# Two attention blocks on one core: division halves, phi(q) chains and other dense chains laid among one another by a new rule, and block A's last q and k ahead of its values

## The chip, the cores and the metric

The kernel runs on one core of a Trainium2 chip. The metric is the device time of one execution in microseconds; the median of three runs of the kernel before is 288.62 us (287.77, 288.62 and 296.04). Profiles are of one profiled execution, and all places in time below count from the first instruction of that execution.

## The reference

Two blocks with inputs of their own, each with x of 2048 tokens by 640, wqkv of 640 by 1920 and wo of 640 by 640, all bf16. Both have 32 heads of 20. Block A is causal attention in a sliding window of 256 keys; block B is linear attention.

```python
# A: q, k, v = split(x @ wqkv)
scores = einsum("bhqd,bhkd->bhqk", q, k) * 20 ** -0.5
scores = where((0 <= i - j) & (i - j < 256), scores, -1e9)
a = (softmax(scores) @ v) @ wo
# B: q, k, v = split(x @ wqkv)
phi = lambda t: where(t > 0, t + 1, exp(t)) + 1e-6
kv = einsum("bhsd,bhse->bhde", phi(k), v);  z = sum_s phi(k)
num = phi(q) @ kv;  den = phi(q) . z + 1e-6
b = (num / den) @ wo
out = concatenate([a, b], axis=-1)
```

## The kernel before

The tokens are cut into four superblocks of 512. The order of the instructions on every engine is the order in which the program writes them; no scheduler moves them.

**The main loop** walks over 90 units, numbered 0 to 89: units 0 to 17 belong to superblock 0 of block A, 18 to 41 to superblock 1, 42 to 65 to 2, 66 to 89 to 3. A unit writes the scores of one tile on TensorE (`scores`, line 485: keys by queries for four heads, into the one S_ps buffer of four banks), their Exp on ScalarE (line 493, one instruction of 128x2048), and the masks on GpSimd (line 507). The values of a tile (`values`, line 529, 16 short matmuls) are written two units after its scores. In every third unit VectorE normalizes the result of a group of four heads (lines 551 and 552). After that, each unit takes dense matmuls from a generator called `fill` for as many columns as a constant rate gives it (334,400 columns over 90 units, so 3,716 a unit), so dense matmuls stand between the values of one unit and the scores of the next. What the rate leaves over is written behind unit 89, and then the last output projection of block A (`a_out_last`).

**The dense work** comes in chains. A chain is a row of accumulating matmuls into one PSUM bank; a pool `dps` gives three banks to all of them, and when a chain is written it takes a bank that is free at that place of the program. One engine's step or more then reads the bank, and only after the last of them can another chain use it. The kinds, with the letters used below:

- E: a q or k chain of block A (`a_qk`, five matmuls of 512 columns, line 194), evicted by one copy on VectorE (`evac`, line 185). Two of these groups, of five chains each, make q and k of a superblock. They go to DRAM and come back in a padded layout (`bounce`: a write, and four reads for each of q and k, on SP's queue).
- V: a value chain (`v_proj`, five matmuls of 320 columns), evicted in the same way.
- Q: a phi(q) chain of block B (`b_q`, five of 512 columns). `phi` reads the bank twice: an Exp on ScalarE (line 203), and, after a step on the Exp's result (line 207), a VectorE step that takes the larger of the input and 0 and adds the Exp (line 210). These two VectorE steps are not written at once: they wait in a list `later`, and `flush` writes them behind the next eviction, phi or division.
- N: a division half (`b_num`, half of the heads for 128 tokens, three short matmuls against kv_bd, line 436). VectorE adds 1e-6 to the denominators, takes reciprocals and multiplies (lines 445, 448, 449), and the bank is free after the multiplication. After both halves of 128 tokens a DMA transposes the result (otokB) into oT_B, on SP's queue. A superblock has eight halves. oT_B takes the buffers of block A's xA, of which there are two.
- O: an output chain (`wo_proj`, four of 512 columns by five, then one bank with the 128 columns left of all four token blocks, 20 short matmuls), evicted by one copy on VectorE; the finished superblock goes out by a DMA on GpSimd's queue.

Each generator ends a chain by yielding an `End`, and gives a count of columns before it for each matmul. `even(a, na, b, nb, lead)` alternates the chains of two generators: `nb` chains of `b` evenly among `na` chains of `a`, `b` first where `lead` is set. In `fill`, `early` stands for block A's last values and then its last q and k (superblock 3); `outs` for the output projections of superblocks 0 to 2, A and B by turns. The part of `fill` that the change touches begins behind `b_kv(3)`, the last sum of phi(k) and values, in unit 43.

Of the kernel before, what the change touches and what calls it, by code (L numbers as in the profile page):

```python
# [9 lines left out]
P = 128  # L10
# [11 lines left out]
TPS = SB // P  # L22
# [30 lines left out]
def kernel(  # L53
# [10 lines left out]
    nc = tc.nc  # L64
    _, S, D = A_x.shape
    KT = D // P
# [109 lines left out]
    def flush():  # L176

        while later:
            later.pop(0)()

    def evac(dst, src, to=None):
        if to == "A":
            nc.scalar.activation(out=dst, in_=src, func=ACT.Copy)
        else:
            nc.vector.tensor_copy(out=dst, in_=src)  # L185
        flush()

    def bank():
        return dps.tile([P, SB], F32, name="dense")

    def chain(dst, lhs, rhs, n):

        for kt in range(KT):
            nc.tensor.matmul(  # L194
                dst, lhsT=lhs(kt), rhs=rhs(kt), start=(kt == 0), stop=(kt == KT - 1)
            )
            if kt < KT - 1:
                yield n

    def phi(dst, src, view=lambda t: t[:]):  # L200

        e = sp.tile([P, SB], BF16, name="e")
        nc.scalar.activation(out=view(e), in_=src, func=ACT.Exp)  # L203
        flush()

        def rest():
            nc.vector.tensor_scalar(  # L207
                out=e[:], in0=e[:], scalar1=1e-6, scalar2=1.0 + 1e-6, op0=ALU.add, op1=ALU.min
            )
            nc.vector.scalar_tensor_tensor(  # L210
                out=dst, in0=src, scalar=0.0, in1=view(e), op0=ALU.max, op1=ALU.add
            )

        later.append(rest)
# [4 lines left out]
    def even(a, na, b, nb, lead=False):  # L219


        def one(g):
            for c in g:
                yield c
                if isinstance(c, End):
                    break

        done = 0
        for i in range(na):
            while lead and done < nb and done * na <= i * nb:  # L230
                done += 1
                yield from one(b)
            yield from one(a)
            while not lead and done * na < (i + 1) * nb:
                done += 1
                yield from one(b)
        yield from a


    xA, xB = {}, {}  # L240
    q_pad, k_pad, v_tok = {}, {}, {}
# [3 lines left out]
    def bounce(n, s, st, dst):  # L245


        scratch = tc.dram_tile([D, SB], BF16, name=f"{n}_scr{s}")
        eng = nc.scalar if s == 0 else nc.sync
        eng.dma_start(out=scratch.rearrange("(c p) n -> p c n", p=P), in_=st[:])  # L250
        sv = scratch.rearrange("(g j d) n -> j d g n", j=4, d=DH)

        def reads():
            for j in range(4):
                nc.sync.dma_start(out=dst[32 * j : 32 * j + DH, :, :], in_=sv[j])

        return reads

    def a_qk(s, between=()):
        for n, base in (("q", 0), ("k", D)):  # L260
            st = stp.tile([P, KT, SB], BF16, name="st")
            for c in range(KT):
                ps = bank()
                yield from chain(
                    ps[:],
                    lambda kt: w_sb["A"][:, kt, base + c * P : base + (c + 1) * P],
                    lambda kt: xA[s][:, kt, :],
                    SB,
                )
                evac(st[:, c, :], ps[:])  # L270
                if c == KT - 1:
                    pad, pl, name = (q_pad, qp, "qpad") if n == "q" else (k_pad, kp, "kpad")
                    pad[s] = pl.tile([P, NG, SB], BF16, name=name)
                    if n == "q":
                        q_reads = bounce(n, s, st, pad[s])
                        for g in between:
                            yield from g
                    else:
                        late_reads[s] = bounce(n, s, st, pad[s])
                        q_reads()  # L280
                yield End(SB)

    def hook(gen, n, fn):

        for i, c in enumerate(gen):
            if i == n:
                fn()
            yield c

    def v_proj(n, xt, dst):  # L290
        hh = H // 2
        for tb in range(TPS):
            for i in range(2):
                ps = bank()
                yield from chain(
                    ps[:, 0 : hh * DH],
                    lambda kt: xt[:, kt, tb * P : (tb + 1) * P],
                    lambda kt: w_sb[n][:, kt, 2 * D + i * hh * DH : 2 * D + (i + 1) * hh * DH],
                    hh * DH,
                )  # L300
                evac(
                    dst[:, tb, i * hh : (i + 1) * hh, 0:DH],
                    ps[:, 0 : hh * DH].rearrange("p (h d) -> p h d", d=DH),
                )
                yield End(hh * DH)

    def a_v(s):
        v_tok[s] = vp.tile([P, TPS, H, HV], BF16, name="vA")
        nc.gpsimd.memset(v_tok[s][:, :, :, DH:HV], 1.0)
        yield from v_proj("A", xA[s], v_tok[s])  # L310
# [86 lines left out]
    for i in range(2):  # L397
        parts = []
# [7 lines left out]
    oT_B = {}  # L406
# [3 lines left out]
    def b_q(s):  # L410
        xt = xB[NS + s]
        pq = pqp.tile([P, KT, SB], BF16, name="phi")
        pq_of[s] = pq
        for c in range(KT):
            ps = bank()
            yield from chain(
                ps[:],
                lambda kt: w_sb["B"][:, kt, c * P : (c + 1) * P],
                lambda kt: xt[:, kt, :],
                SB,  # L420
            )
            phi(pq[:, c, :], ps[:])
            yield End(SB)

    def b_num(s):
        flush()
        pq = pq_of[s]
        oT_B[s] = xp.tile([P, KT, SB], BF16, name="xA")
        for tb in range(TPS):
            ot = rp.tile([P, D], BF16, name="otokB")  # L430
            for i in range(2):
                ps = bank()
                ov = ps[:, 0 : hh * HV].rearrange("p (h e) -> p h e", e=HV)
                parts = half_parts[i]
                for n, (c, ho, nh, col) in enumerate(parts):
                    nc.tensor.matmul(  # L436
                        ov[:, col : col + nh, :],
                        lhsT=pq[:, c, tb * P : (tb + 1) * P],
                        rhs=kv_bd[:, c, ho : ho + nh, :],
                        start=(n == 0),  # L440
                        stop=(n == len(parts) - 1),
                        skip_group_check=True,
                    )
                den = sp.tile([P, hh, 1], F32, name="denB")
                nc.vector.tensor_scalar_add(
                    out=den[:], in0=ov[:, :, DH:HV], scalar1=1e-6
                )
                nc.vector.reciprocal(out=den[:], in_=den[:])
                nc.vector.tensor_tensor(  # L449
                    out=ot[:, i * hh * DH : (i + 1) * hh * DH].rearrange(  # L450
                        "p (h e) -> p h e", e=DH
                    ),
                    in0=ov[:, :, 0:DH],
                    in1=den[:].to_broadcast([P, hh, DH]),
                    op=ALU.mult,
                )
                flush()
                yield End(3 * 150)
            nc.sync.dma_start_transpose(
                out=oT_B[s][:, :, tb * P : (tb + 1) * P], in_=ot[:]  # L460
            )

    def b_out(s):
        yield from wo_proj("B", oT_B[s], s, D)
# [102 lines left out]
    def a_out(s):  # L567
        yield from wo_proj("A", oT_A[s], s, 0)
# [29 lines left out]
    def seq(*gens):  # L598
        for g in gens:
            yield from g  # L600
# [23 lines left out]
    def k_reads(s, gen):  # L624
        return hook(gen, 8, lambda: late_reads[s]())

    early = seq(a_v(3), a_qk(3))
    outs = seq(a_out(0), b_out(0), a_out(1), b_out(1), a_out(2), b_out(2))
    fill = seq(
        a_qk(1, between=(load("B", 1),)),  # L630
# [10 lines left out]
        k_reads(2, a_v(2)),  # L641
        b_kv(3),
        load("B", NS + 1),
        even(b_q(0), KT, early, 2),
        load("B", NS + 2),
        even(b_num(0), 2 * TPS, early, 2 * TPS, lead=True),
        early,
        k_reads(3, b_q(1)),
        load("B", NS + 3),
        even(b_num(1), 2 * TPS, outs, 2 * TPS, lead=True),  # L650
        even(b_q(2), KT, outs, 2),
        even(b_num(2), 2 * TPS, outs, 2 * TPS, lead=True),
        even(b_q(3), KT, outs, 2),
        even(b_num(3), 2 * TPS, outs, 2 * TPS, lead=True),
        outs,
        b_out(3),
    )
# [60 lines left out]
```

## Time and profile before

| | |
|---|---|
| median of the runs | 288.62 us |
| the profiled execution | 289.15 us |
| its span, first to last instruction | 287.3 us |
| TensorE busy | 272.2 us (95%) |
| ScalarE busy | 199.9 us (70%) |
| VectorE busy | 181.4 us (63%) |
| GpSimd busy | 163.9 us (57%) |
| granted TensorE clock | 1.000 |
| start of units 43, 47, 60, 70, 89 | 146.94, 157.71, 191.69, 217.65, 267.28 |

A unit's start is the start of its first scores matmul in the order of time. Busy times of TensorE count a matmul from its start to a modelled end; matmuls overlap, so a row of five with 512 columns starts one every 0.216 us though each is listed with 0.38.

### The profile page before, as it was taken

To read this page: it belongs to the slowest core of one execution; us is meant where nothing else is said; L and a number is where in the kernel's file an instruction comes from. 1 tells how busy PE (TensorE), PEld (TensorE's weight loads), DVE (VectorE), ACT (ScalarE), POOL (GpSimd) and SP (SyncE) were. 2 spreads that over 40 slices of the span, in tenths; PEclk is the share of its full clock that TensorE was granted. 3 is DMA by queue.
4 is the path that set the end of the run, shared out by engine and by line. 5 is a ranking of instruction groups with operands and counts; after the bars stand their busy time and mean duration, and the time that the engine had idled before them with its cause. 6 is when DMAs were issued, how large, how long until landed. Compare 5 with 4: busy or idle time off the path is not lost.

```text
span 287.3 us, 8258 instructions
## 1 busy us (share of the span) xinstructions
PE 272.2 (95%) x3512; PEld 157.1 (55%) x3512; DVE 181.4 (63%) x409; ACT 199.9 (70%) x227; POOL 163.9 (57%) x212
## 2 busy tenths in 40 slices
PE   7999988998999999999998989998999999999995
PEld 7644554664665654565664644444555464545653
DVE  0666645756765754546664885457867787677861
ACT  2000058987989888879988768897788878986402
POOL 2000039666666666776689646665766767665620
PEclk9999999999999999999999999999999999999999
DMA  7997699999272062273053542179954155022576
GB/s 247 292 321 202 163 248 176 281 144 159 63 112 59 17 94 94 62 149 67 3 116 72 114 48 72 45 171 134 145 127 72 56 86 138 3 94 48 133 167 204
DMA packets 66676, 35.91 MB, mean 125 GB/s; under 512 B 50800, under 2 KB 65264, under 8 KB 66640
## 3 DMA queue, kind: packets, MB, share of 16 engines
q1 hardware_dynamic: 63792, 27.04, 46.7%
q0 software_dynamic: 1536, 7.05, 9.0%
q10 hardware_dynamic: 1312, 1.31, 1.4%
q8 instruction: 27, 0.44, 0.7%
q14 instruction: 9, 0.07, 0.1%
HBM read 12.45 MB, written 10.49 MB: 80 GB/s over the span
## 4 chain that ended last, share of the span: by engine, by line
PE 71%; DVE 8%; DMA 6%; ACT 6%; POOL 5%; issue 2%; SPq 0%; POOLq 0%
PE dense L194 45%; PE O_ps L529 13%; PE S_ps L485 9%; ACT p L493 4%; POOL p L507 3%; DMA k_scr<-st 2%; DMA kpad<-k_scr 2%; DMA oT<-otokA 2%; PE dense L146 1%; DVE phi L210 1%; DVE otokA L552 1%; DVE osb L185 1%; PE dense L377 1%; POOL kv_bd L163 1%; PE dense L436 1%
## 5 line engine op out<-in xcount | busy, mean ns | idle before, releaser
L507 POOL TENSOR_SCALAR_AFFINE_SELECT p<-p 128x512 bf16<-128x512 bf16 (+2 forms) x178 | 148.1, 833 | 108.1 <-ACT p L493 100.6
L493 ACT ACTIVATE p<-S_ps 128x2048 bf16<-128x2048 f32 x90 | 168.8, 1875 | 49.4 <-PE S_ps L485 49.1
L529 PEld LDWEIGHTS <-p 128*128 128x128 bf16 x1440 | 42.4, 96 | 20.8 <-issue 15.8
L529 PE MATMUL O_ps<-vA,p 128*128 128x21 bf16 x1440 | 51.1, 173 | 1.9 <-POOL p L507 1.9
L194 PE MATMUL dense<-wB,xB 128*128 128x320 bf16 (+2 forms) x320 | 49.2, 298 | 0.1
L194 PE MATMUL dense<-xA,wA 128*128 128x512 bf16 x200 | 46.1, 379 | 0.0
L185 DVE CAST st<-dense 128x512 bf16<-128x512 f32 x40 | 27.4, 690 | 19.9 <-PE dense L194 19.5
L485 PE MATMUL S_ps<-qpad,kpad 20*128 20x256 bf16 (+2 forms) x736 | 36.3, 269 | 2.6 <-issue 1.3
L185 DVE CAST osb<-dense 128x512 bf16<-128x512 f32 (+1 forms) x39 | 25.2, 647 | 15.6 <-PE dense L194 15.5
L194 PEld LDWEIGHTS <-xA 128*128 128x128 bf16 x320 | 26.4, 97 | 15.7 <-issue 1.5
L194 PEld LDWEIGHTS <-xB 128*128 128x128 bf16 x320 | 26.1, 97 | 13.0 <-issue 1.1
L485 PEld LDWEIGHTS <-kpad 20*128 20x128 bf16 x736 | 13.2, 92 | 32.7 <-issue 30.6
L194 PEld LDWEIGHTS <-wA 128*128 128x128 bf16 x200 | 18.4, 97 | 19.7
L210 DVE SCALAR_TENSOR_TENSOR phi<-dense,e 128x512 bf16<-128x512 f32 x40 | 27.7, 692 | 1.4
L194 PE MATMUL dense<-woA,oT 128*128 128x512 bf16 (+1 forms) x160 | 25.8, 299 | 2.7 <-DVE osb L185 1.6
L478 ACT ACTIVATE p<-ident 1x1 bf16<-1x1 bf16 x90 | 16.9, 188 | 15.4 <-DVE st L185 15.4
L194 PE MATMUL dense<-xB,wB 128*128 128x512 bf16 x100 | 25.6, 378 | 0.7 <-DVE phi L210 0.5
L194 PE MATMUL dense<-wA,xA 128*128 128x320 bf16 x160 | 24.9, 299 | 1.4 <-DVE otokB L449 0.8
L194 PE MATMUL dense<-woB,xA 128*128 128x512 bf16 (+1 forms) x160 | 25.3, 298 | 0.5 <-PE dense L436 0.4
L207 DVE TENSOR_SCALAR e<-e 128x512 bf16<-128x512 bf16 x40 | 19.1, 477 | 10.5 <-ACT e L203 10.4
L203 ACT ACTIVATE e<-dense 128x512 bf16<-128x512 f32 x40 | 23.4, 593 | 0.5 <-PE dense L194 0.2
L185 DVE CAST vB<-dense 128x320 bf16<-128x320 f32 x32 | 15.2, 489 | 12.3 <-PE dense L194 11.8
(36 smaller groups left out, 159.9 us busy)
## 6 DMA issues: line engine op xcount, KB each, us to landing
out_dram<-osb POOLq DMA_DIRECT2D x7, 640.0 KB, 3.9
qpad<-q_scr SPq DMA_DIRECT2D x16, 160.0 KB
kpad<-k_scr SPq DMA_DIRECT2D x16, 160.0 KB
wA<-in_A_wqkv_dram SPq DMA_DIRECT2D x3, 800.0 KB
q_scr<-st SPq DMA_DIRECT2D x3, 640.0 KB
k_scr<-st SPq DMA_DIRECT2D x3, 640.0 KB
wB<-in_B_wqkv_dram SPq DMA_DIRECT2D x2, 800.0 KB
wB<-in_B_wqkv_dram POOLq DMA_DIRECT2D x1, 800.0 KB, 11.5
```

The costliest lines, as they stand in the source:

```text
L146: nc.tensor.matmul(ps[:, 0:P], lhsT=ident[:], rhs=ident[:], start=True, stop=True)
L163: nc.gpsimd.affine_select(out=v, in_=v, pattern=[[-sgn * DH, nh], [0, HV]], compare_op=ALU.is_ge, fill=0.0, base=base, channel_multiplier=sgn,
L185: nc.vector.tensor_copy(out=dst, in_=src)
L194: nc.tensor.matmul(dst, lhsT=lhs(kt), rhs=rhs(kt), start=(kt == 0), stop=(kt == KT - 1))
L203: nc.scalar.activation(out=view(e), in_=src, func=ACT.Exp)
L207: nc.vector.tensor_scalar(out=e[:], in0=e[:], scalar1=1e-6, scalar2=1.0 + 1e-6, op0=ALU.add, op1=ALU.min)
L210: nc.vector.scalar_tensor_tensor(out=dst, in0=src, scalar=0.0, in1=view(e), op0=ALU.max, op1=ALU.add)
L478: nc.scalar.activation(out=p_all[0:1, 4 * SB : 4 * SB + 1], in_=ident[0:1, 0:1], func=ACT.Copy)
L485: nc.tensor.matmul(S_ps[:, j, blk * P : blk * P + n], lhsT=kt[32 * j : 32 * j + DH, g, ko : ko + P], rhs=q_pad[s][32 * j : 32 * j + DH, g, ...
L493: nc.scalar.activation(out=p, in_=S_ps[:], func=ACT.Exp, scale=scale)
L507: nc.gpsimd.affine_select(out=v, in_=v, pattern=[[0, 4], [0, b1 - b0], [sgn, P]], compare_op=ALU.is_ge, fill=0.0, base=0 if kind == "D" el ...
L529: nc.tensor.matmul(O_ps[:, slot, j, :], lhsT=p[:, j, b * P : (b + 1) * P], rhs=v_tok[kb // TPS][:, kb % TPS, 4 * gg + j, :], start=(first ...
```

## The change

A new function `mix` takes several generators with a number of chains and an offset each, and writes their chains in the order of (chain number + offset) / number of chains. A generator marked `True` is emptied afterwards. The part of `fill` behind `b_kv(3)` uses it in place of `even`: the five Q chains of a superblock now stand among the division halves of the superblock before it and other chains, where they had followed behind those halves. Block A's last q and k come ahead of its last values, and the reads of k are written eight matmuls into those values. The transposing DMA of a pair of halves is written right after the second half's multiplication, where it had been written when the generator was next asked for a chain.

```diff
+    def mix(*parts):
+        order = sorted(
+            ((i + off) / n, k) for k, (_, n, off, _) in enumerate(parts) for i in range(n)
+        )
+        for _, k in order:
+            for c in parts[k][0]:
+                yield c
+                if isinstance(c, End):
+                    break
+        for g, _, _, whole in parts:
+            if whole:
+                yield from g
...
     (b_num)
                 flush()
+                if i == 1:
+                    nc.sync.dma_start_transpose(
+                        out=oT_B[s][:, :, tb * P : (tb + 1) * P], in_=ot[:]
+                    )
                 yield End(3 * 150)
-            nc.sync.dma_start_transpose(
-                out=oT_B[s][:, :, tb * P : (tb + 1) * P], in_=ot[:]
-            )
...
-    early = seq(a_v(3), a_qk(3))
+    early = seq(a_qk(3), k_reads(3, a_v(3)))
     outs = seq(a_out(0), b_out(0), a_out(1), b_out(1), a_out(2), b_out(2))
...
         b_kv(3),
         load("B", NS + 1),
-        even(b_q(0), KT, early, 2),
+        mix((b_q(0), KT, 0.1, True), (early, 3, 0.5, False)),
         load("B", NS + 2),
-        even(b_num(0), 2 * TPS, early, 2 * TPS, lead=True),
-        early,
-        k_reads(3, b_q(1)),
+        mix((b_num(0), 2 * TPS, 0.1, True), (b_q(1), KT, 0.5, True), (early, 15, 0.4, True)),
         load("B", NS + 3),
-        even(b_num(1), 2 * TPS, outs, 2 * TPS, lead=True),
-        even(b_q(2), KT, outs, 2),
-        even(b_num(2), 2 * TPS, outs, 2 * TPS, lead=True),
-        even(b_q(3), KT, outs, 2),
-        even(b_num(3), 2 * TPS, outs, 2 * TPS, lead=True),
+        mix((b_num(1), 2 * TPS, 0.1, True), (b_q(2), KT, 0.5, True), (outs, 8, 0.4, False)),
+        mix((b_num(2), 2 * TPS, 0.1, True), (b_q(3), KT, 0.5, True), (outs, 9, 0.4, False)),
+        mix((b_num(3), 2 * TPS, 0.1, True), (outs, 8, 0.6, False)),
         outs,
         b_out(3),
```

The order in units 61 to 64, with the number of matmuls of each chain that falls into the unit (t stands for an O chain's last bank with 20 short matmuls):

| unit | before | after |
|---|---|---|
| 61 | O4 N3 O3 | O5 Q3 |
| 62 | O2 N3 O4 | Q2 N3 O4 |
| 63 | O1 N3 O5 | O1 N3 Q5 |
| 64 | N3 t20 N3 O1 | O5 N3 O2 |

## The prediction

> **What bounds the kernel now.** I read the page first: TensorE is busy 95% of the span, but that is an average in which a waiting matmul counts too.
>
> ```profile
> PE 272.2 (95%) x3512; PEld 157.1 (55%) x3512; DVE 181.4 (63%) x409; ACT 199.9 (70%) x227; POOL 163.9 (57%) x212
> ```
>
> So I went to the order of time on the engines in the stretch that the change rearranges, and followed one unit after another by its first scores matmul. Here are units 72 (start 223.34) and 73 (225.71), with the start of 74; columns: start, duration in us, engine, line, operation, in square brackets the idle time before it.
>
> ```profile
> 223.34 0.40 PE L485 MATMUL S_ps<-qpad,kpad 20*128 20x384 bf16 x8
> 223.78 1.88 ACT L493 ACTIVATE p<-S_ps 128x2048 bf16<-128x2048 f32 x1
> 224.30 1.24 PE L194 MATMUL dense<-woA,oT 128*128 128x512 bf16 x5
> 225.38 0.33 PE L436 MATMUL dense<-kv_bd,phi 128*128 128x147 bf16 x3
> 225.56 0.59 ACT L203 ACTIVATE e<-dense 128x512 bf16<-128x512 f32 x1
> 225.58 0.69 DVE L185 CAST osb<-dense 128x512 bf16<-128x512 f32 x1 [0.25 <-PE dense L194]
> 225.71 0.40 PE L485 MATMUL S_ps<-qpad,kpad 20*128 20x256 bf16 x8
> 226.18 0.37 DVE L207 TENSOR_SCALAR e<-e 128x512 bf16<-128x512 bf16 x1
> 226.46 1.24 PE L194 MATMUL dense<-woA,oT 128*128 128x512 bf16 x5
> 226.59 0.69 DVE L210 SCALAR_TENSOR_TENSOR phi<-dense,e 128x512 bf16<-128x512 f32 x1
> 227.19 0.16 DVE L445 TENSOR_SCALAR denB<-dense 128x16 f32<-128x16 f32 x1
> 227.39 0.25 DVE L448 RECIPROCAL denB<-denB 128x16 f32<-128x16 f32 x1
> 227.53 0.33 PE L436 MATMUL dense<-kv_bd,phi 128*128 128x84 bf16 x3
> 227.68 0.49 DVE L449 TENSOR_TENSOR otokB<-dense,denB 128x320 bf16<-128x320 f32 x1
> 228.23 0.61 PE L194 MATMUL dense<-woA,oT 128*128 128x512 bf16 x2 [0.37 <-DVE otokB L449]
> 228.77 0.40 PE L485 MATMUL S_ps<-qpad,kpad 20*128 20x128 bf16 x8
> ```
>
> Two limits show. **The floor**: the scores have one buffer, so scores, their Exp 0.44 later (1.88 us), and the next scores form a loop: 0.44 + 1.88 + 0.05 = 2.37, unit 72's length (225.71 - 223.34). **The dense part**: scores and values take 0.75, dense matmuls start then, and with about 0.1 to the next scores a unit cannot be shorter than 0.85 plus its dense matmuls (0.216 us for 512 columns, by the starts of a row of them). Most units hold 1.44 to 1.5 us of dense work and fit under the floor; one of 1.71 lasts 2.56. **On top come stalls**: unit 73 lasted 3.06, because the last chain waited 0.37 (0.53 against the usual start-to-start time) for a bank held by the division half before it, which stood on VectorE behind the second half of a phi. In the wait view of TensorE from 150 us on, such waits are the large entries:
>
> ```profile
> PE dense L194 <- DVE otokB L449: 1.8, 4, 0.6
> PE dense L194 <- DVE osb L185: 1.7, 3, 1.0
> ```
>
> With "unit = the larger of 2.38 and 0.85 + dense" the 46 units 43 to 88 would take 111.1 us. From the starts of units 43 (146.94) and 89 (267.28) they took 120.3. The 9.2 between are stalls: 1.26 in unit 45 (masks of kv_bd on GpSimd ahead of the scores' masks) and 8.0 in units 47 to 88: 2.4 in units 47 to 49 (division halves alternating with A's value chains), 1.15 in 61, 0.6 each in 64 and 73, 0.75 in 70, 1.5 in 84 and 85, the rest in small ones. That is all a reordering can win here.
>
> **The change part by part.** It adds and removes no arithmetic; the columns up to unit 89 stay, and the tail after it keeps its order. What it changes is which chain takes which of three banks, and when that bank comes free. As built, a chain takes the bank whose last reader came first in the program. By the starts in the rows, VectorE spends on an output or q/k eviction 0.60 (ready after 0.69, 0.2 behind the chain), on a value eviction 0.40, on a division half 0.89, on a phi 0.41 + 0.61 once its Exp is done, on A's normalization 0.70. The Exp of a phi(q) chain ending in a unit can't run before that unit's own scores' Exp ends (0.05 before the next unit), so it is ready some 0.55 into the next unit, and its second VectorE step ends 1.1 to 1.7 into it; that step is written behind the next chain's eviction. So a Q holds a bank for most of a unit, and the other chains take turns in two.
>
> *Q chains spread (gains and costs).* Before, the Qs stood together, and the halves ran with outputs in three banks (O N O N, each awaiting the third before). Now Q, N and O alternate, and two patterns appear. Pattern one: O, N, O', where O' awaits O's bank, because the third is a Q's. N is 0.16 us of TensorE and the eviction needs 0.2 + 0.69, so about 0.75 is lost when no unit border lies between. The order before has it at 159.88, 196.97, 228.23 and 255.53, costing 0.39, 1.12, 0.53 and 0.78 against the usual pace. The order after has it in units 48, 58 (value chain), 64, 70, 75, 79, 81: laid out with the durations above they lengthen their units by 0.71, 0.52, 0.70, 0.81, 0.70, 1.29 (A's normalization comes first there), 0.80, sum 5.5. Pattern two: a chain that awaits a Q's bank, or an N whose division stands behind a Q's phi: units 56, 59, 61, 63, 67, 69, 73, 76, by 0.53, 0.82, 0.10, 0.54, 0.80, 0.28, 0.76, 0.21, sum 4.0. For example unit 67: phi's second step of the Q of units 65 and 66 ends 1.69 into the unit (Exp from 0.05 before it to 0.54 in it, then 0.41 and 0.69 on VectorE), its bank is wanted at 0.91 and got at 1.74. The same way of laying out gives the units 72 to 77 of before as 2.43, 3.05, 2.41, 2.38, 2.63, 2.43; the trace has 2.38, 3.06, 2.40, 2.38, 2.63, 2.53.
>
> *What goes:* nearly all of the 8.0. The Q-free end (units 84 to 88) is laid out without a stall, and a 0.25 stall at 269.75 goes from the tail. *Unit 45* keeps its 1.26: kv_bd is made at the same place. *Unit borders:* the new order has 111.4 instead of 111.1 without stalls.
>
> *A's q and k ahead of its values.* The q/k chains end in unit 54 instead of 57, the eight reads are issued by unit 56, some 24 us before unit 66 needs them; before, the reads came at unit 58 and nothing waited for them late. The values come at unit 60 instead of 50, first read at 68. Both ends hidden by some 19 us or more: nothing, and if the cover were gone the wait would be a whole read, 5.85 us in the chain that ended last (k of superblock 0). The memset on GpSimd (0.67) goes with the values; the masks take 1.85 behind an Exp that ends 2.32 into its unit, and the values want them 0.32 into the second unit after, which leaves 2 x 2.37 + 0.32 - 4.17 = 0.89: between nothing and 0.67, taken as nothing.
>
> *The otokB transposes* are issued one chain earlier on SP's queue. For superblock 2 the first waits for b_out(0)'s last chain (under 1 us), for 3 for b_out(1)'s (units 81 to 83, 5 us); behind it stand only transposes of the same tile, wanted after unit 89. Nothing; the 4 outputs on GpSimd move with their chains, 0.77 each, under the same 0.89.
>
> **The sum**, by stretches of units, before to after: 43-46 10.77 to 10.95; 47-59 33.98 to 34.07; 60-69 25.96 to 26.6; 70-88 49.63 to 50.55; tail -0.25: together +1.6. The profiled execution took 289.15 (span 287.3 and 1.85 around it), so 290.75 by it; it lies 0.5 above the median of 288.62, so **290.2** for the median.
>
> **Rivals.** *Smoothing works* (0.14): before, VectorE is crowded where halves meet outputs or values and slack where Qs stand; spread evenly, the stalls shrink. For it: the 2.4 us in units 47 to 49 surely go. Against: VectorE's load was not the wait in pattern one, the border of two banks was. If pattern two gives nothing and pattern one its smallest row (7 x 0.39 = 2.7), stalls fall from 8.0 to 2.7: 288.6 - 5.1 = 283.5. The Trainium skill, Perfetto Trace Analysis, Optimization Strategy under Identifying Performance Opportunities, says that interleaving stretches bound by different engines may help; by that rule this rival is the result. *Slower, past 2%* (0.07): ScalarE falls behind, so that a Q's Exp starts after the next unit's scores' Exp instead of before it. Place: units 48 to 78 with 15 Qs; price up to 1.88 each, of which some 0.5 is left after slack: 15 x 0.5 = 7.5, 297.7 in all. It decides once a unit holds more Exp than it lasts; with one Q it holds 1.88 + 0.19 + 0.59 = 2.66 of stated durations against 2.38, but Qs come in about every second unit (2.37 a unit), so it is near, not past. *The stalls only trade places* (0.14): 288.6 give or take 0.8.
>
> **How the numbers follow.** The forecast (0.65) is 289.2 to 292.0. Unknown sizes: pattern one lies between 7 x 0.39 and 7 x 1.12 (-2.8 to +2.3 about my 5.5), pattern two between nothing and twice 4.0; I take the layout since it met the rows. Both ends together are unlikely, which leaves 286.8 to 293.2 as the range, with part of the first rival below it and the second above. About 2% is what a measurement of this kernel tells from no change: faster (below 282.85) 0.05, within 0.88, slower (above 294.4) 0.07.
>
> **What would show it.** In the new profile: waits of dense matmuls on VectorE (osb, st, otokB, phi) above those of before; units 48, 64, 70, 75, 79, 81 of 3.1 us or more, most Q-free ones at 2.38; units 47 to 59 about as long as before; no wait on kpad, vA or qpad. Wrong if pattern one is missing, or if ScalarE's Exp of phi stands a unit late.

## The result, and the profile after

| | before | after |
|---|---|---|
| median of seven runs each | 289.45 us | 291.72 us |
| lowest and highest | 287.77, 296.04 | 290.03, 297.89 |
| the profiled execution | 289.15 | 291.21 |
| its span | 287.3 | 289.5 |

The ratio of after to before is 1.0102, with a 95% interval of 1.0064 to 1.0140. The change makes the kernel about 1% slower: within 2%, and yet clear of no change. The ratio leaves out the executions of either kernel that lie over 1.5% above its fastest (of after 297.89, at a granted clock of 0.988), which the medians hold. By stretches of units, from the starts of the units in the order of time:

| stretch | before | after, forecast | after, measured |
|---|---|---|---|
| start of the span to unit 43 | 146.94 | 146.94 | 146.56 |
| units 43 to 46 | 10.77 | 10.95 | 11.27 |
| units 47 to 59 | 33.98 | 34.07 | 34.11 |
| units 60 to 69 | 25.95 | 26.6 | 27.19 |
| units 70 to 88 | 49.64 | 50.55 | 50.66 |
| behind the start of unit 89 | 20.04 | 19.79 | 19.72 |

Units 43 to 88 together went from 120.34 to 123.23; below, "the stretch" means these. Without stalls the new order would need 111.4, so 11.8 us of it are stalls now (9.2 before).

The busy times on the page of after say nothing of that; they are those of before within 0.4 us.

```profile
PE 271.9 (94%) x3512; PEld 156.9 (54%) x3512; DVE 181.0 (63%) x409; ACT 200.3 (69%) x227; POOL 163.8 (57%) x212
```

The wait view of TensorE from 150 us on does say it (engine, line, what it waited for: us in total, times, the longest):

```profile
PE dense L194 <- DVE osb L185: 3.5, 5, 1.1
PE dense L194 <- DVE phi L210: 1.8, 4, 0.5
PE O_ps L545 <- POOL p L523: 1.0, 2, 0.6
PE dense L194 <- DVE otokB L464: 1.0, 2, 0.6
PE dense L194 <- DVE st L185: 0.8, 2, 0.6
```

The same view of the kernel before has, beside the two rows that the prediction shows:

```profile
PE O_ps L529 <- POOL p L507: 1.0, 2, 0.6
PE dense L194 <- DVE phi L210: 0.5, 1, 0.5
```

Waits on output evictions (osb) went from 1.7 to 3.5 us, on phi from 0.5 to 1.8, on q/k evictions (st) from no entry among the rows to 0.8; those on division halves (otokB) fell from 1.8 to 1.0. The values' wait for the masks (O_ps on GpSimd's p) is 1.0 in both.

The order of time of after shows the two patterns. Unit 67 begins at 210.52; columns as in the prediction:

```profile
210.36 0.59 ACT L203 ACTIVATE e<-dense 128x512 bf16<-128x512 f32 x1
210.52 0.40 PE L501 MATMUL S_ps<-qpad,kpad 20*128 20x256 bf16 x8
210.99 0.37 DVE L207 TENSOR_SCALAR e<-e 128x512 bf16<-128x512 bf16 x1 [0.53 <-ACT e L203]
211.26 0.33 PE L451 MATMUL dense<-kv_bd,phi 128*128 128x84 bf16 x3
211.39 0.69 DVE L210 SCALAR_TENSOR_TENSOR phi<-dense,e 128x512 bf16<-128x512 f32 x1
212.14 1.24 PE L194 MATMUL dense<-woB,xA 128*128 128x512 bf16 x5 [0.55 <-DVE phi L210]
213.74 0.40 PE L501 MATMUL S_ps<-qpad,kpad 20*128 20x128 bf16 x8
```

This is pattern two: the output chain could have run behind the half at 211.26, but its bank is a Q's, read by the phi until 212.08. The unit lasts 3.22. And unit 79, pattern one with A's normalization (recA, otokA) in front, which lasts 3.71 (its start at 243.49, scores of unit 80 at 247.19):

```profile
243.49 0.40 PE L501 MATMUL S_ps<-qpad,kpad 20*128 20x256 bf16 x8
244.24 0.38 PE L194 MATMUL dense<-woA,oT 128*128 128x128 bf16 x4
244.42 0.26 DVE L567 RECIPROCAL recA<-O_ps 128x16 f32<-128x16 f32 x1 [2.39 <-PE O_ps L545]
244.46 0.33 PE L451 MATMUL dense<-kv_bd,phi 128*128 128x147 bf16 x3
244.71 0.49 DVE L568 TENSOR_TENSOR otokA<-O_ps,recA 128x320 bf16<-128x320 f32 x1
245.12 0.68 DVE L185 CAST osb<-dense 128x512 bf16<-128x512 f32 x1
245.86 1.24 PE L194 MATMUL dense<-woB,xA 128*128 128x512 bf16 x5 [1.07 <-DVE osb L185]
247.19 0.40 PE L501 MATMUL S_ps<-qpad,kpad 20*128 20x128 bf16 x8
```

O ends, N is written in 0.33, and O' needs the bank of O, whose eviction starts only behind the normalization: TensorE stands still for 1.07 us.

### The profile page after: what moved, and what is told of

It reads as the page before. It is cut to its first block, busy times and chain, and to the rows that moved or that the text cites. A ratio compares the mean times of both kernels' runs of the same rounds, so it can differ in the third digit from the quotient of the medians.

```text
span 289.5 us, 8249 instructions
## 1 busy us (share of the span) xinstructions
PE 271.9 (94%) x3512; PEld 156.9 (54%) x3512; DVE 181.0 (63%) x409; ACT 200.3 (69%) x227; POOL 163.8 (57%) x212
## 4 chain that ended last, share of the span: by engine, by line
PE 74%; DVE 9%; POOL 5%; ACT 5%; issue 4%; DMA 2%; ACTq 0%; POOLq 0%
PE dense L194 49%; PE O_ps L545 12%; PE S_ps L501 9%; ACT p L509 3%; POOL p L523 3%; DVE phi L210 2%; DMA oT<-otokA 2%; ACT e L203 1%; PE dense L146 1%; DVE e L207 1%; DVE osb L185 1%; PE dense L392 1%; POOL kv_bd L163 1%; DVE otokA L568 1%; PE dense L451 1%
## 5 line engine op out<-in xcount | busy, mean ns | idle before, releaser
L194 PEld LDWEIGHTS <-xA 128*128 128x128 bf16 x320 | 26.6, 97 | 17.9 <-issue 3.3
L194 PE MATMUL dense<-xB,wB 128*128 128x512 bf16 x100 | 26.9, 378 | 1.3 <-DVE phi L210 1.0
L567 DVE RECIPROCAL recA<-O_ps 128x16 f32<-128x16 f32 (+1 forms) x34 | 8.5, 249 | 23.9 <-PE O_ps L545 23.7
L185 DVE CAST vB<-dense 128x320 bf16<-128x320 f32 x32 | 15.2, 489 | 12.2 <-PE dense L194 11.8
```

Source lines behind the costliest of these rows:

```text
L194: nc.tensor.matmul(dst, lhsT=lhs(kt), rhs=rhs(kt), start=(kt == 0), stop=(kt == KT - 1))
L567: nc.vector.reciprocal(out=r[:, 0:n, :, :], in_=O_ps[:, :, :, DH:HV])
```

## The experiments

**Theory:** the banks. A Q holds one of three for most of a unit, so chains laid beside it have two, and each O, N, O' or each chain that comes round to a Q's bank waits. **Rivals:** the amount of VectorE's work in the stretch (it evicts, divides and does the phis, and the new order may crowd it); or another part of the change than the laying of Qs among halves. All ratios below are to the kernel before, run beside the experiment on the same chip.

### Which part of the change: the other parts alone, and the Qs put back together

The kernel before, with only A's q and k ahead of its values and the early transposing DMA:

```diff
+                if i == 1: nc.sync.dma_start_transpose(...)   # in b_num, behind flush()
-    early = seq(a_v(3), a_qk(3))
+    early = seq(a_qk(3), k_reads(3, a_v(3)))
...
-        k_reads(3, b_q(1)),
+        b_q(1),
```

> The kernel before with the two small parts of the change alone: A's last q and k ahead of its values (k's reads eight matmuls into the values), and the transposing DMA written right behind the second half. The chains stay in the old alternation. Theory: the DMAs are hidden in both orders, and the only effect is that the halves of superblock 0 now alternate with q and k chains (1.08 us on TensorE against 0.60 on VectorE) instead of values (0.68 against 0.40): the 2.4 us of stalls in units 47 to 49 fall to about 1, 0.995 of before. Rival (the placement of q and k or of the transposes is what costs time in the changed kernel): 1.005 to 1.01.

Measured: 288.17 us, ratio 0.9930 (0.9879 to 0.9980); the stretch 119.96. Units 47 to 59 lost 0.85 us (33.13) and units 43 to 46 gained 0.49, the same as in after. So these parts do not make after slower. They help a little, by 0.38 us in the stretch (most of the ratio's 0.7% lies elsewhere: unit 43 starts at 146.34 instead of 146.94, which these parts do not touch). Before, the division halves alternated with A's value chains in units 47 to 49, and here with the q and k chains. The prediction had put this part at nothing. What `mix` does beyond these parts costs 123.23 - 119.96 = 3.3 us.

Then after, with the Qs of the last three superblocks behind the mixed halves instead of among them:

```diff
-        mix((b_num(0), 2 * TPS, 0.1, True), (b_q(1), KT, 0.5, True), (early, 15, 0.4, True)),
+        mix((b_num(0), 2 * TPS, 0.1, True), (early, 15, 0.4, True)),
+        b_q(1),
...
(and so for b_num(1) with b_q(2), b_num(2) with b_q(3))
```

> The changed kernel with one part undone: the phi(q) chains of the next superblock are not laid among the halves but follow them together; halves of superblock 0 still stand among all 15 remaining q, k and value chains, and the halves of 1 and 2 among 8 and 9 outputs. Theory (the spread phi(q) chains cause the cost): almost every chain awaits the third before it again; what stays is unit 45 (1.26), the first half in unit 48 (0.7) and about 1.5 where phi(q) chains give way to halves: 3.5 us of stalls in units 43 to 88 against 9.2 before, 0.982 of before. Rival (VectorE's work): halves and outputs alternate as densely as before in units 61 to 67, so those stretches stall as before, 0.995 to 1.0. If the cost were in A's order or in the DMAs: 1.01.

Measured: 288.62 us, ratio 0.9974 (0.9938 to 1.0010); the stretch 119.59. So 3.6 us of after's stretch come from the Qs among the halves, but the expectation was missed in size: it had 3.5 us of stalls left, 114.9 in all, so less than half of the gain over after came. Units 71 to 77, halves and outputs in turn with no Q open, ran at 2.38 to 2.59, while the windows view has VectorE busy for 13.48 of those 16.96 us, a larger share (79%) than in units 70 to 79 of after, the third superblock's halves with Qs among them (19.06 of 28.07, 68%). The loss is elsewhere: where a block of five Qs gives way to halves. Unit 61 took 4.22, unit 70 4.30, units 80 to 82 2.79, 3.00 and 3.16. The order of time of unit 61 of this kernel:

```profile
191.26 1.08 ACT L203 ACTIVATE e<-dense 128x512 bf16<-128x512 f32 x2
191.41 0.40 PE L501 MATMUL S_ps<-qpad,kpad 20*128 20x256 bf16 x8
192.29 0.69 DVE L210 SCALAR_TENSOR_TENSOR phi<-dense,e 128x512 bf16<-128x512 f32 x1
193.03 1.24 PE L194 MATMUL dense<-woA,oT 128*128 128x512 bf16 x4 [0.72 <-DVE phi L210]
193.45 0.69 DVE L210 SCALAR_TENSOR_TENSOR phi<-dense,e 128x512 bf16<-128x512 f32 x1
194.20 0.33 PE L451 MATMUL dense<-kv_bd,phi 128*128 128x84 bf16 x3
195.09 0.61 PE L194 MATMUL dense<-woA,oT 128*128 128x512 bf16 x2 [0.57 <-DVE otokB L464]
195.63 0.40 PE L501 MATMUL S_ps<-qpad,kpad 20*128 20x128 bf16 x8
```

Two phis are still open when the outputs begin (the Exps at 191.26 count two), so the first output waits 0.72 for one bank, and a half's bank keeps the second waiting 0.57. A block of Qs doesn't avoid the price of a long-held bank; it collects it at its end.

### The order alone: the same chains, laid out by the units

If the order is all, another order of the same chains should beat both kernels. Units were laid out as in the prediction (durations from the rows, the bank of each chain, VectorE in the order of the program) for many orders, and the shortest was taken. The loads of B's x go with the Qs. In the string, q, n and o are Q, N and O chains, e the next chain of `early`:

```diff
-        mix(...)            # all five calls of mix
+        lay("qeqqeeqqeeneenenneeenneeneenqeqqqqeennoononononononqoqoqoqqoonononnoonnonoqonqoqqqoononononononnoon"),
         outs,
```

> The same chains, instructions and DMAs as the changed kernel, in an order of the chains behind the last kv sum that was chosen by laying the units out with the durations of the rows, so that few chains meet a bank that is still held: the phi(q) chains alternate with outputs or q and k chains instead of with halves, and the halves alternate with outputs by themselves. The chains from there, q for phi(q), n for a half, e for A's q, k and values, o for an output chain: qeqqeeqqeeneenenneeenneeneenqeqqqqeennoononononononqoqoqoqqoonononnoonnonoqonqoqqqoononononononnoon. Theory (which chains are next to one another decides, through the banks): from unit 43 to unit 89 114.9 us against 120.3 in the kernel before and 123.2 in the changed one, 0.98 of before. Rival (VectorE's amount of work per stretch): the same work in the same stretch, so 119 to 123 us and 0.99 to 1.01.

Measured: 283.63 us, ratio 0.9803 (0.9746 to 0.9860); the stretch 115.21. The order takes 8.0 us out of the stretch of after, with the same instructions. The wait view of TensorE from 150 us on, its first rows:

```profile
PE O_ps L545 <- POOL p L523: 1.0, 2, 0.6
PE dense L194 <- DVE phi L210: 0.5, 1, 0.5
PE dense L194 <- DVE osb L185: 0.4, 1, 0.4
```

Osb fell from 3.5 to 0.4 and phi from 1.8 to 0.5. In this order Qs come one to four at a time, mostly with long chains between or behind them, and most halves stand in turn with outputs where no Q is open.

### What holds the bank: its reader or VectorE's load

The first try: in after, and in the kernel before, the second step of phi(q) reads an f32 tile in SBUF instead of the bank, so that the Exp is the bank's last reader. The tile is kv_acc, which holds sums of phi(k) and values that are finished by then; the larger of q and 0 is left out of phi(q).

```diff
+    nc.gpsimd.memset(kv_acc[:], 0.5)
...
-                out=dst, in0=src, ...
+                out=dst, in0=src if second is None else second, ...   # second: 512 columns of kv_acc, for phi(q)
```

> The changed kernel, with one edit: in phi(q) the second VectorE step reads a constant f32 tile in SBUF in place of the PSUM bank. This leaves out a part of the computation (the larger of q and 0 in phi(q) is replaced by a constant); all instructions stay, and the bank of a phi(q) chain is free once ScalarE's Exp has read it, instead of after the two VectorE steps behind the next eviction. Theory (phi(q) chains hold one of three banks for most of a unit, and halves and outputs wait for one another in the other two): of the 9 us of stalls beyond unit 45's, some 8 go, 0.98 of the kernel before, about 8 us below the changed kernel; units 64, 70, 75, 79 and 81 return to 2.38 to 2.56. Rival (VectorE's work per unit is what delays the chains, whoever holds a bank): VectorE has the same instructions, so the time stays at 1.010 of before, within 1 us of the changed kernel.

> The same edit in the kernel before (the larger of q and 0 in phi(q) left out in the same way). Theory: the phi(q) chains stand together there and cost less, so only the stalls at the border of phi(q) chains and halves go (units 61, 70, 73, 84): some 3 to 4 of 8 us, 0.988 of before; the halves that alternate with A's values (units 47 to 49, 2.4 us) stay. So the order of the two kernels turns round: the changed one is the faster once the bank is free. Rival (VectorE's work): no change, 1.000, and the changed order stays 1% slower.

Measured: after with it 294.14 us, ratio 1.0166 (1.0056 to 1.0275), the stretch 122.50; before with it 295.55, ratio 1.0232 (1.0159 to 1.0306), the stretch 123.52. Both expectations were missed in the total, which tells nothing of the banks, since the stand-in isn't a step of the same length. The source view of that line, after with the edit (durations in ns: shortest, median, longest; first and last start):

```profile
L210 DVE SCALAR_TENSOR_TENSOR phi<-dense,e x20: 690/691/692, 44.7 to 147.3; 128x512 bf16<-128x512 f32 x20
L210 DVE SCALAR_TENSOR_TENSOR phi<-kv_acc,e x20: 691/1100/1531, 155.2 to 256.3; 128x512 bf16<-128x512 f32 x20
```

With the bank as its input the step takes 0.69 always; with two inputs in SBUF 0.69 to 1.53. And both executions have a stop of TensorE of 5.3 us near 57, of which more below; it lies ahead of the stretch and inside the ratios, so the ratios say nothing of the edit. Unit by unit the theory fares better than in the total. With the stand-in in after, units 48, 64, 69, 75, 79 and 81 took 2.37, 2.52, 2.38, 2.38, 2.62 and 2.52, down from 3.08, 3.29, 3.00, 3.08, 3.71 and 3.30; with it in the kernel before, units 61, 70 and 84 took 2.79, 2.61 and 2.38 instead of 3.65, 3.31 and 3.08. What the banks gave was lost again in units such as 62 (3.52 in after with it, 5.09 in before with it) and 73 (4.06 and 3.90).

The second try keeps the bank out of the second step with a step of one input. The larger of q and 0 is again left out of phi(q).

```diff
+            if kind == "free":          # phi(q)
+                nc.vector.tensor_scalar(
+                    out=dst, in0=view(e), scalar1=0.0, scalar2=0.0, op0=ALU.max, op1=ALU.add)
+                return
```

> The changed kernel, where phi(q)'s second VectorE step works on the Exp's result in SBUF with one input alone, so that nothing but ScalarE's Exp reads a phi(q) bank. It leaves out the larger of q and 0 in phi(q). Earlier the stand-in was a two-input step with an f32 input from SBUF, which took 1.02 us against 0.69; a one-input bf16 step (0.37 to 0.48 in the rows) is to avoid that. VectorE loses 20 x 0.2 = 4 us of work. Theory (the held bank): units 63, 67, 69 and 73 return to 2.38 to 2.56, units 43 to 89 fall from 123.2 to 119 to 120 us. Rival (amount of VectorE work): a gain in proportion to the 4 us, half of what the next kernel gains.

Measured: four runs between 285.31 and 293.09 us, too few for an interval, so the profile is read alone: the stretch 119.31, 3.9 less than after's and as expected. The new step took 0.66 us on average against 0.69, and VectorE's busy time is 178.9 against after's 181.0; what changed is when the bank comes free. Units 63 and 69 fell to 2.38, 75 to 2.38, 64 and 81 to 2.52, 79 from 3.71 to 2.62: the stalls of both patterns. Not all stalls went: 59, 67 and 70 kept 3.24, 3.18 (its rows are shown in the last section) and 3.17, and 62 (3.17), 73 (3.65), 80 (3.16) and 82 (2.91) grew. In the wait view from 150 us on no wait for a phi is left; its first rows are:

```profile
PE dense L194 <- DVE otokB L469: 1.8, 3, 0.7
PE dense L194 <- DVE osb L185: 1.5, 2, 1.0
```

In units 67 and 73 the new step took 1.13 us, and the eviction that TensorE waits for stands behind it. So 3.9 us of after's 11.8 go with the long hold of a Q's bank, net of what the longest of the new steps cost.

Then the rival, from two sides. VectorE with less work in after: phi(q) without its first step (the 1e-6 and the limit at 1 are left out), 20 instructions.

```diff
-            nc.vector.tensor_scalar(out=e[:], in0=e[:], scalar1=1e-6, ...)
+            if kind != "less":          # not in phi(q)
+                nc.vector.tensor_scalar(out=e[:], in0=e[:], scalar1=1e-6, ...)
```

> The changed kernel with the first VectorE step of phi(q) left out (the 1e-6 and the limit at 1 in phi(q) are left out). VectorE loses 20 x 0.41 = 8.2 us of work, twice what the kernel with the free bank loses, but the second step still reads the bank, 0.41 earlier. Theory (the held bank): each wait behind a phi(q) shrinks by 0.41 at most, and the waits of an output for an output (units 48, 64, 70, 75, 79, 81) stay: units 43 to 89 take 120.5 to 121.5 us, a smaller gain than with the bank free. Rival (amount of VectorE work): the larger gain of the two, some 6 us.

VectorE with more work: a reciprocal, whose result nobody uses, behind each half's multiplication, 32 of 0.253 us as listed.

```diff
                 (b_num, behind the multiplication)
+                nc.vector.reciprocal(out=den[:], in_=den[:])
                 flush()
```

> The changed kernel with one VectorE step more in each division half: the reciprocal of the denominators once more behind the multiplication, in place on SBUF, its result unused; the bank of the half is free before it. 32 x 0.29 = 9.3 us of VectorE work are added. Theory (banks): VectorE has room in most units, and only where the added step stands ahead of an awaited one does it cost up to 0.29: units 43 to 89 take 125 to 126.5 us, 2 to 3 us more. Rival (amount of VectorE work): nearly all of the 9.3 us shows, 130 to 132 us.

Measured: with less work 288.80 us, ratio 0.9983 (0.9945 to 1.0021), the stretch 120.34; with more work 290.97, ratio 1.0049 (1.0001 to 1.0097), the stretch 123.26, which is after's 123.23. The page's busy times, of the one with less and then of the one with more:

```profile
PE 272.0 (95%) x3512; PEld 157.3 (55%) x3512; DVE 172.1 (60%) x389; ACT 200.2 (70%) x227; POOL 163.3 (57%) x212
```

```profile
PE 272.8 (94%) x3512; PEld 157.8 (55%) x3512; DVE 185.9 (64%) x441; ACT 200.1 (69%) x227; POOL 163.3 (57%) x212
```

And the wait view of TensorE from 150 us on, of the one with more:

```profile
PE dense L194 <- DVE osb L185: 3.5, 5, 1.1
PE dense L194 <- DVE phi L210: 1.6, 4, 0.5
```

The added reciprocals come to 8.1 us as listed, and VectorE's busy time rose by almost 5 (other steps came out shorter). That cost nothing in the stretch, against an expectation of 2 to 3: unit 62 took 0.24 more (2.93) and unit 63 0.24 less (2.66, its phi's first step at 0.28 instead of 0.79), and elsewhere the reciprocals fell where VectorE had time. 9 us less gained 2.9, nearly all of it where the work taken away stood between a Q and its bank: units 59, 67 and 73 got 0.4 shorter, 63 and 69 went to 2.38, while the pattern one units kept their lengths (48 3.08, 64 3.30, 70 3.30, 75 3.08, 79 3.70, 81 3.30). Unit 62 gained 0.25 because the step had stood ahead of A's normalization. The kernel with the free bank, with 2 us less on VectorE, gained more (3.9) than this one with 9 us less. The amount of VectorE's work is not the cause; the two steps of a phi are, where a bank waits for them, and so is the border of two banks.

### A stop of TensorE that no wait explains

In the order of time of the kernel before, TensorE stops in the middle of a scores tile, with nothing to wait for ("issue"):

```profile
66.18 0.21 PE L485 MATMUL S_ps<-qpad,kpad 20*128 20x128 bf16 x1
67.70 0.40 PE L485 MATMUL S_ps<-qpad,kpad 20*128 20x128 bf16 x7 [1.31 <-issue]
```

After has it too (1.50 behind the same matmul, the 605th of the records in both), so it makes no more than 0.2 of the difference. In the two kernels with the SBUF stand-in it came at the 472nd and was larger; after with the stand-in:

```profile
56.18 0.57 PE L194 MATMUL dense<-wB,xB 128*128 128x320 bf16 x3
62.06 2.29 PE L194 MATMUL dense<-wB,xB 128*128 128x320 bf16 x8 [5.32 <-issue]
```

There the windows view has the granted clock at 0.64 in the 4 us from 58 on and at 0.50 in the next 4. Meanwhile a transposing load of x of block A takes 17.68 us on SP's queue in the kernel before, from 46.30 to 63.98, where the other loads by that line take 2.7 to 8.4:

```profile
46.30 17.68 SPq L114 DMA_TRANSPOSE xA<-in_A_x_dram  x1
```

Two edits of the kernel before move traffic away from that place. One issues the late weight loads 14 units later, the other puts the load of A's third superblock behind the first sum of phi(k) and values:

```diff
-        if i == 0:
+        if i == 14:
             late_loads()
```

```diff
-        load("A", 2),
         b_kv(0),
         load("B", 2),
+        load("A", 2),
```

> A side question that the traces raised: in most of them TensorE stands once for 1.2 to 5.6 us between 56 and 68 us with nothing to wait for in the profile, always at the same count of its instructions (about 1,217, in two kernels 956), while the DMA engines are busiest. Here the kernel before issues its three late weight loads (2.4 MB on GpSimd's queue, from 42.5 us on) in unit 14 instead of unit 0, about 75 us; no other edit. If that traffic delays whatever TensorE then lacks, the gap goes or moves to about 75 to 95 us, and the runs 1 to 5 us above the rest become rare: 0.995 of before. If not, the gap stays at its count with its length: 1.000. The prediction's theory has no stake in it.

> The same question with the other large transfer of that time: the kernel before, where the transposing load of A's third superblock (on SP's queue from 46 us on, 17.7 us at the head of it) comes behind the first kv sum instead of ahead of it, some 20 us later. If this load is what delays TensorE, the gap between 56 and 68 us goes: 0.995 of before. If not: 1.000, or slower where the load comes too late for what needs it.

Measured: the weights later 289.78 us, ratio 1.0007 (0.9959 to 1.0055), and a stop of 0.72 us remains, at 58.06. The transposing load later 287.44 us, ratio 0.9961 (0.9932 to 0.9991); no stop, units 10 to 19 took 24.84 us instead of 26.37. Its ten runs lie between 286.82 and 288.90, while the 19 of the kernel before beside them lie between 287.44 and 295.26. Here is the place in the order of time, a scores tile of one piece:

```profile
67.59 0.40 PE L485 MATMUL S_ps<-qpad,kpad 20*128 20x128 bf16 x8
```

So the place of that load bears on the stop. Three other experiments, with the load where it was, show no stop in their one profile (the Qs together, the bank free, more work on VectorE), though the load takes as long there (17.67 us with the Qs together), so it doesn't come in every execution.

That the load holds up the fetching of TensorE's instructions is argued, not shown, but the traces lean that way. The page of the kernel before lists, among the DMA queues, one for instructions (packets, MB, share):

```profile
q8 instruction: 27, 0.44, 0.7%
```

Counted in the trace, its packets from 76.77 to 110.98 start after 1497, 1725, 1991, 2253 and 2495 of TensorE's 7024 matmuls and weight loads, one for about 250; the stop stands behind 1211 of them in before and after and behind 955 with the weights later, 256 apart. In all eight profiles with a stop a packet of this queue starts 1.4 to 1.6 us behind the end of the transposing load on SP's queue (65.52 behind 63.98 in the kernel before); in the three with the load in its place and no stop it starts at 61.5 to 61.9, while the load still runs. One thing doesn't fit: in the three profiles where the stop came near 57, it ended ahead of that packet (at 62.06 against 64.93 in after with the stand-in). So the cause of the stop stays open.

### Both together

The order laid out by the units and the later transposing load, in after:

> The order laid out against held banks, and the transposing load of A's third superblock behind the first kv sum, together. Theory (banks, and the load that holds up TensorE once): the two gains are in different stretches and add: units 43 to 89 as in the laid-out order, 115.2 us, no gap without a wait between 56 and 68 us; 0.975 to 0.98 of before, some 282 us, and no run far above the rest. If the gap had gone by chance in the kernel with the load moved: about 283.6, with single runs near 288.

Measured: 282.20 us (281.95 to 282.62), ratio 0.9728 (0.9680 to 0.9776), faster than both kernels; the stretch is again 115.21. Units 10 to 19 took 24.85, without a stop, and the six runs lie within 0.7 us, where those of the laid-out order alone go from 282.37 to 287.81.

## Why the prediction was right, and where its sizes were off

It said 290.2 us, 1.6 more than before, mostly from units 60 to 88; the profiled execution took 2.06 more (291.21 against 289.15). As a ratio that is 0.55% forecast and 1.0% measured, and the forecast lies just under the interval (0.64% to 1.40%). The total is in part luck: the stretch grew by 2.89 where 1.83 was forecast, and 0.38 of that excess is hidden because the units ahead of 43, which the change doesn't touch, came out shorter. Two workings are slightly off as written, and neither moves the forecast: in unit 67, 0.54 + 0.41 + 0.69 is 1.64, not 1.69 (the trace has 1.56), and 8.0 - 2.7 in the first rival is 5.3, not 5.1.

- **The floor and the dense part** held. The Q-free units 83 to 88 took 2.38, 2.52, 2.38, 2.52, 2.38 and 2.38, as laid out.
- **Pattern one** held in place and in size: units 48, 58, 64, 70, 75, 79 and 81 took 3.08, 2.89, 3.29, 3.29, 3.08, 3.71 and 3.30, each within 0.1 of its layout.
- **Pattern two** held in place: units 56, 59, 63, 67, 73 and 76 took 2.94, 3.22, 2.90, 3.22, 3.22 and 2.68, within 0.1 as well, and 61 took 2.57, 0.09 under its layout. **Unit 69 was mis-sized**: 3.00 instead of 2.66. The term that failed is "a phi 0.41 + 0.61". The first step took 0.80 here, as the order of time of after shows, beside two masks of GpSimd (the last section has more of this):

```profile
216.15 1.84 POOL L523 TENSOR_SCALAR_AFFINE_SELECT p<-p 128x1024 bf16<-128x1024 bf16 x2 [1.08 <-ACT p L509]
216.59 0.80 DVE L207 TENSOR_SCALAR e<-e 128x512 bf16<-128x512 bf16 x1
217.42 0.69 DVE L210 SCALAR_TENSOR_TENSOR phi<-dense,e 128x512 bf16<-128x512 f32 x1
218.17 1.02 PE L194 MATMUL dense<-xB,wB 128*128 128x512 bf16 x4 [0.54 <-DVE phi L210]
```

  The 0.39 more of that step are the 0.34 that the unit was longer, and without the step (the experiment with less work) unit 69 took 2.38. Unit 77 was 0.22 over its layout, behind a step of 0.65. In unit 63 the step took 0.79 too, but the Exp ahead of it ended 0.12 into the unit instead of the 0.55 laid out, since unit 62 was longer; there the two errors made up for each other.
- **Two stalls were missed.** In unit 46 a Q waits at 157.30 for a q/k eviction that stands behind A's normalization on VectorE (the unit took 2.89 instead of 2.58), which is what makes units 43 to 46 0.50 longer instead of 0.18. In unit 62 the values wait 0.33 for the normalization of the group before (otokA). With unit 69 that is 0.65, and units 60 to 69 were 0.6 over the forecast.
- **A's q and k ahead, the transposes, the memset at nothing**: no scores or values wait for kpad, qpad or vA from 150 us on (the one entry that names vA, 0.4 in unit 58, is a dense chain that awaits the bank of a value chain: pattern one), and the masks cost the values 1.0 us as before. Only that the q and k chains are better neighbours for the halves than the values was missed (0.85 in units 47 to 59 when done alone); in after it is part of the layout of those units, whose sum was right.
- **The tail** gave 0.32 instead of 0.25; the units ahead of 43, which the change doesn't touch, 0.38 that were not forecast. The measured differences add up: 0.50 + 0.13 + 1.24 + 1.02 - 0.32 - 0.38 = 2.2, the difference of the spans.

The rivals: *smoothing works* is out for this order, and so is its premise, since VectorE's load moved by -9 or +5 us leaves pattern one where it is. The Trainium skill, Perfetto Trace Analysis, Optimization Strategy under Identifying Performance Opportunities, says that interleaving regimes may help; the runs show both sides of that, 1.010 with chains laid evenly and 0.980 with the same chains laid by who holds a bank. *ScalarE falls behind* did not come about: its Exps of phi(q) stand at the unit borders, as at 210.36 above, and no wait of a scores tile for ScalarE is among the entries. *The stalls only trade places* is nearly what happened to the phi and otokB waits, but not to osb.

## What to carry to other kernels

Where short chains share a few banks with chains whose bank is held long, count what is left: one long-held bank of three leaves two, and a short chain between two long ones then costs almost a whole eviction (0.5 to 1.3 us here), whatever the busy shares say. Neither spreading the long-held ones evenly (1.010) nor putting them in a block (0.997) is right as such; laying the units out from the durations of the trace, and choosing the order by that, was worth 2% (0.980). Test a load theory by adding load: 5 us more on the engine that the waits name cost nothing in the stretch here.

## What was not expected of the hardware

**Two kinds of VectorE step from SBUF end only after GpSimd's instruction has ended.** The first step of a phi took 0.28 to 0.86 us in after. The step of the experiment with the free bank, also bf16 from SBUF to SBUF, took 0.29 to 1.13; here is one, in unit 67 of that kernel (start 207.32), in the order of time, with the masks it ran beside and what waited in the end:

```profile
207.34 1.84 POOL L528 TENSOR_SCALAR_AFFINE_SELECT p<-p 128x512 bf16<-128x512 bf16 x2 [0.53 <-ACT p L514]
208.20 1.13 DVE L211 TENSOR_SCALAR phi<-e 128x512 bf16<-128x512 bf16 x1
209.25 0.68 DVE L185 CAST osb<-dense 128x512 bf16<-128x512 f32 x1
209.98 0.59 PE L194 MATMUL dense<-xB,wB 128*128 128x512 bf16 x2 [0.50 <-DVE osb L185]
```

GpSimd's second mask ends at 209.18, and the step 0.15 later. Its length is its own 0.29, plus the 0.98 that GpSimd's instruction had left, less 0.14. The same sum gives all 20 lengths of this step within 0.01 us, where GpSimd had more than 0.14 left, and the stand-in's, f32 and bf16 from SBUF: 0.69 alone, 1.11 with 0.57 left, 1.53 with 0.99 left. It doesn't hold for all of VectorE's steps from SBUF: the reciprocal of the denominators, f32 in SBUF, took 0.25 in all 32 cases of after, of which 20 started beside a GpSimd instruction. The steps that read the bank took 0.69 throughout, beside GpSimd or not. The Trainium skill, SBUF — State Buffer, section "SBUF: two separate sides", says that VectorE (in its two-port modes or with two inputs in SBUF) and GpSimd share a pair of ports as an exclusive lock, held for a whole instruction; these lengths agree with a lock, and not with a shared bandwidth.

**TensorE's stop.** 1.0 to 1.6 us behind the same matmul of the program in the kernels where it came at 66, 0.7 and 5.3 behind earlier ones in three others, and none with the transposing load moved, nor in three profiles with it in place. The Trainium skill, Runtime: NRT & Kernel Launch, section "Instruction fetch mechanics", says that instructions are fetched by DMA in blocks while the engine runs and that the cost is mostly hidden; if these stops are such fetches, which no run here proves, it was not hidden behind a long transposing load.
